# A two-branch attention kernel: 192 transposes moved from TensorE to a DMA queue, half sums on GpSimd, PV in sets of three, another start and end

## The chip, the cores and the metric

One core of a Trainium2 chip. The metric is the device time of one execution in microseconds (us), median of several executions. A change of less than 2% counts as no change.

## The reference, cut to what matters

Two attention branches read the same x (2048 x 512) and are mixed by a gate:

```python
# branch A: linear attention, 32 heads of 16
phi_q = concat([softmax(pq), softmax(-pq)])      # 32 features per head
phi_k = concat([softmax(pk), softmax(-pk)])
o = (phi_q @ (phi_k.T @ v)) / (phi_q @ phi_k.sum(tokens) + 1e-6)
# branch B: exact softmax attention, 32 heads of 16
p = softmax(q @ k.T * Dh ** -0.5);  o = p @ v
# out = g * (oA @ woA) + (1 - g) * (oB @ woB),  g = sigmoid((x * gate_w).sum(-1))
```

Branch B has 32 x 2048 x 2048 exponentials. The kernel cuts them in 2048 tiles of 128 x 512.

## The kernel before

ScalarE takes the exponentials of most tiles, in "slots" of three or two tiles (one activation for 1536 or 1024 columns). VectorE does the rest by bit tricks, partly with GpSimd. TensorE computes scores (`qk_mm`), PV, and the projections, and runs matmuls with zeros that are meant to hold its clock up. Branch A runs beside it. A planner inside the kernel (a list scheduler with a duration for each operation) fixes **the order of every engine** when the kernel is built. At run time each engine follows its order and waits on semaphores; if one entry waits, everything behind it on that engine waits (the lines of the changed kernel below show 3.84 us of such a wait on TensorE).

Transfers inside SBUF go to one queue, that of SyncE, at priority -40. The planner believes that each takes 0.07 us of the queue:

```python
def moves(kind, fn, n, reads, writes, name, lat=2.0):
    ...
    op = P.add("sp", 0.07 * n, -40, fn, reads=reads, writes=writes, name=name, sem=chain[kind][0], lat=lat)
```

Branch A's queries, 16 tiles of 128 tokens (cut). `fill` adds matmuls into a PSUM bank, `drain` what empties it:

```python
def q_rest(i, prio):
    b = i % 2
    mms = [... e.transpose(ap.bitcast(BF16)[:, 128*g:128*(g+1)], phiQ[:, b, 128*g:128*(g+1)], ident[:]) for g in range(8)]
    f, mm = fill(prio, mms, [("phiQ", b), "ident"], name=f"T{i}", ...)
    drain(f, mm, "dve", 0.69, prio, ... tensor_copy(phiQT[:, b, :, :], ap...), writes=[("phiQT", b)])
    for rnd in range(2):
        ...   # "N": 4 matmuls phiQT x kzbd (numerator and denominator), then VectorE writes oA
    mms = [... e.transpose(..., oA[:, b, 128*t:128*(t+1)], ident[:]) for t in range(KT)]       # KT = 4
    ...
    drain(f, mm, "dve", 0.42, prio, ... tensor_copy(oAT[:, i, :, :], ap...), writes=[("oAT", i)])
```

The normaliser of branch B uses SyncE's queue: after the last PV of a pair of heads the result leaves PSUM (tile Tf), its denominators go out and come back spread over the partitions (ld, Lq, lr, Rb), and GpSimd multiplies. In the trace oAT appears under the name phiK, whose memory it uses.

The softmax here doesn't subtract the row's maximum and nothing guards it: scores larger than these inputs give would overflow.

## Time and profile before

The profile that came with the kernel had caught an execution at about a quarter of TensorE's speed (the prediction shows its lines: matmuls of 512 columns stand 0.84 us apart). A second profile of the same kernel, taken with the first experiments, ran at full speed: there they stand 0.43 us apart in the warm-up and 0.22 us near the end (four from 778.05 to 778.91), at a mean granted clock of 0.993. First its page: span, busy times, busy tenths of ScalarE in 40 slices, the chain that ended last, and the group of the exponentials (its last columns are ScalarE's idle time before them and what ended it).

```profile
span 785.6 us, 15391 instructions
PE 726.2 (92%) x6304; PEld 227.5 (29%) x6304; DVE 681.8 (87%) x1125; ACT 762.4 (97%) x712; POOL 316.4 (40%) x273
ACT  5989999999999999999999999999999999999995
ACT 80%; PE 11%; DVE 5%; issue 1%; DMA 1%; SPq 1%; POOL 0%
L833 ACT ACTIVATE E_t<-psS 128x1536 bf16<-128x1536 f32 (+1 forms) x641 | 733.4, 1352 | 8.6 <-PE psS L741 6.8
```

ScalarE is busy from the first exponential to the last and owns 80% of the chain. So the prediction's reading, that ScalarE is the bound, holds at full speed. So do its durations of ScalarE: a 1536 and a 1024 back to back take 2.36 us here (from 10.82 on), 2.37 us at a quarter of TensorE's speed. Two pieces of notation: "SPq" is SyncE's queue, and "E_t" are the buffers that hold exponentials until PV has read them. The rest of this document uses four terms whose sum is the span: **head** (up to the first exponential), **floor** (ScalarE's own work, 756.5 us by the prediction's sum), **waits** (first to last exponential, less the floor) and **tail** (from the end of the last exponential). Here the first exponential starts at 10.82 and the last ends at 775.61, so these are 10.8 + 756.5 + 8.3 + 10.0 = 785.6.

### The profile page before, as it was taken

To read this page: it belongs to the slowest core of one execution; us is meant where nothing else is said; L and a number is where in the kernel's file an instruction comes from. 1 tells how busy PE (TensorE), PEld (TensorE's weight loads), DVE (VectorE), ACT (ScalarE), POOL (GpSimd) and SP (SyncE) were. 2 spreads that over 40 slices of the span, in tenths; PEclk is the share of its full clock that TensorE was granted. 3 is DMA by queue.
4 is the path that set the end of the run, shared out by engine and by line. 5 is a ranking of instruction groups with operands and counts; after the bars stand their busy time and mean duration, and the time that the engine had idled before them with its cause. 6 is when DMAs were issued, how large, how long until landed. Compare 5 with 4: busy or idle time off the path is not lost.

```text
span 1905.5 us, 15334 instructions
## 1 busy us (share of the span) xinstructions
PE 1865.0 (98%) x6247; PEld 289.4 (15%) x6304; DVE 695.2 (36%) x1125; ACT 821.8 (43%) x712; POOL 314.5 (17%) x273
## 2 busy tenths in 40 slices
PE   9999999999999999999999999999999999999999
PEld 3111112111211111212111111111111111111111
DVE  1332343333333333334333344443444443432431
ACT  2444444444444444444444444444444444443431
POOL 2010212112121121110222111120111202021200
DMA  4000000000000000100000000000000000000000
GB/s 111 2 3 12 6 4 6 4 9 4 4 6 3 9 3 2 31 3 9 4 4 6 3 10 4 5 7 2 9 4 9 4 4 12 9 7 9 13 9 14
DMA packets 37206, 18.01 MB, mean 9 GB/s; under 512 B 26584, under 2 KB 34136, under 8 KB 37136
## 3 DMA queue, kind: packets, MB, share of 16 engines
q1 hardware_dynamic: 35648, 16.36, 3.7%
q8 instruction: 49, 0.80, 0.2%
q10 hardware_dynamic: 1104, 0.66, 0.1%
q0 software_dynamic: 384, 0.02, 0.0%
q14 instruction: 21, 0.17, 0.0%
HBM read 7.87 MB, written 2.59 MB: 5 GB/s over the span
## 4 chain that ended last, share of the span: by engine, by line
PE 96%; DVE 2%; issue 2%; ACT 0%
PE psO L852 34%; PE psS L741 29%; PE psS L559 8%; PE psM L559 8%; PE psO L843 5%; PE psM L741 4%; PE psM L1097 1%; PE psS L597 1%; PE psS L609 1%; PE psM L609 1%; PE psM L477 1%; DVE Tx_t L799 1%; PE psS L1097 0%; PE psS L1122 0%; PE psM L1104 0%
## 5 line engine op out<-in xcount | busy, mean ns | idle before, releaser
L833 ACT ACTIVATE E_t<-psS 128x1536 bf16<-128x1536 f32 (+1 forms) x641 | 786.2, 1236 | 1009.4 <-PE psS L741 848.5
L741 PE MATMUL psS<-qz_t,kTB_t 32*128 32x512 bf16 x1828 | 659.3, 890 | 14.3 <-issue 3.1
L852 PE MATMUL psO<-E_t,vaug_t 128*32 128x512 bf16 x1602 | 539.7, 861 | 0.8 <-issue 0.8
L741 PE MATMUL psM<-qz_t,kTB_t 32*128 32x512 bf16 x220 | 189.0, 859 | 0.8 <-DVE Tx_t L799 0.8
L799 DVE TENSOR_SCALAR Tx_t<-psM 128x512 int16<-128x512 f32 x125 | 86.2, 690 | 219.3 <-PE psM L741 129.1
L741 PEld LDWEIGHTS psS<-qz_t,kTB_t 32*128 32x128 bf16 x1828 | 71.7, 103 | 603.2 <-issue 400.7
L822 POOL TENSOR_TENSOR Tx_t<-Tx_t,vA_t 128x512 bf16<-128x512 bf16 x88 | 99.3, 1155 | 363.7 <-DVE Ty_t L816 237.3
L799 DVE TENSOR_SCALAR Tx_t<-psS 128x512 int16<-128x512 f32 x125 | 86.1, 689 | 175.5 <-PE psS L741 152.8
L852 PE MATMUL psO<-Tx_t,vaug_t 128*32 128x512 bf16 (+1 forms) x250 | 135.1, 991 | 0.0
L852 PE MATMUL psO<-Ty_t,vaug_t 128*32 128x512 bf16 x250 | 123.6, 1009 | 0.0
L843 PE MATMUL psO<-xT_t,zero_t 128*32 128x512 bf16 x540 | 117.8, 820 | 0.0
L852 PEld LDWEIGHTS psO<-E_t,vaug_t 128*32 128x32 bf16 x1602 | 50.6, 99 | 298.4 <-issue 288.5
L822 POOL TENSOR_TENSOR oT_t<-oT_t,WoB_t 128x512 bf16<-128x512 bf16 x44 | 49.7, 1149 | 207.1 <-DVE oT_t L816 167.4
L1062 POOL TENSOR_TENSOR phiK_t<-EA_t,stat_t 128x1024 bf16<-128x1024 bf16 x16 | 30.8, 1928 | 249.7 <-DVE stat_t L1060 140.3
L852 PE MATMUL psO<-WAT_t,vaug_t 128*32 128x512 bf16 x152 | 69.8, 930 | 0.0
L852 PE MATMUL psO<-vA_t,vaug_t 128*32 128x512 bf16 x104 | 65.0, 962 | 0.0
L1062 POOL TENSOR_TENSOR phiQ_t<-EA_t,stat_t 128x1024 bf16<-128x1024 bf16 x16 | 30.8, 1926 | 187.8 <-DVE vA_t L814 80.8
L822 POOL TENSOR_TENSOR Tx_t<-Tx_t,WoB_t 128x512 bf16<-128x512 bf16 x32 | 36.2, 1151 | 147.1 <-DVE Ty_t L816 68.9
L559 PE MATMUL psS<-Wp_t,xT_t 128*128 128x512 bf16 x60 | 50.7, 971 | 1.5 <-DVE oT_t L816 0.5
L559 PE MATMUL psM<-xT_t,WB_t 128*128 128x512 bf16 x51 | 45.0, 1008 | 5.5 <-issue 4.8
L799 DVE TENSOR_SCALAR WAT_t<-psS 128x512 int16<-128x512 f32 x39 | 26.9, 690 | 63.0 <-PE psS L741 54.0
L559 PE MATMUL psM<-Wp_t,xT_t 128*128 128x512 bf16 x53 | 46.2, 1000 | 2.5 <-issue 1.5
(184 smaller groups left out, 1291.9 us busy)
## 6 DMA issues: line engine op xcount, KB each, us to landing
Rb_t<-lr SPq DMA_DIRECT2D x120, 32.0 KB, 1.8
qz_t<-qz_t SPq DMA_DIRECT2D x120, 16.0 KB, 1.8
Tf_t<-Tf_t SPq DMA_DIRECT2D x60, 32.0 KB, 2.0
out_dram<-WvA_t SPq DMA_DIRECT2D x14, 128.0 KB, 1.7
WB_t<-in_B_wqkv_dram SPq DMA_DIRECT2D x3, 384.0 KB, 4.7
WvA_t<-in_A_wqkv_dram SPq DMA_DIRECT2D x1, 512.0 KB, 4.0
WoA_t<-in_A_wo_dram SPq DMA_DIRECT2D x1, 512.0 KB, 3.5
WoB_t<-in_B_wo_dram SPq DMA_DIRECT2D x1, 512.0 KB, 4.7
```

The source lines that it names most:

```text
L477: ins = e.matmul(psM[:], lhsT=Ebuf[:, 0, 0:128], rhs=Ebuf[:, 0, 0:512], start=True, stop=True)
L559: return [lambda e, ap, i=i: e.matmul(ap, lhsT=lhs[i], rhs=rhs[i], start=(i == 0), stop=(i == len(lhs) - 1)) for i in range(len(lhs))]
L597: mms = [lambda e, ap, i=i, t=t: e.matmul(ap[:, 128 * i:128 * (i + 1)], lhsT=xT[:, t, NQ * c + 128 * i:NQ * c + 128 * (i + 1)], rhs=W_B[:, ...
L609: mms = [lambda e, ap, i=i, t=t: e.matmul(ap[:, 256 * i:256 * (i + 1)], lhsT=xT[:, t, NQ * c + 128 * (2 * hf + i):NQ * c + 128 * (2 * hf + ...
L741: return e.matmul(bank, lhsT=kT_B[32 * i:32 * i + 32, b // 8 % 2, 128 * kt:128 * (kt + 1)], rhs=qz[32 * i:32 * i + 32, b // 2 % 4, b % 2, ...
L799: ops.append(drain(f, mm, "dve", 0.70, d_prio(d), lambda e, ap, q=q: e.tensor_scalar(quarter(tb, q).bitcast(I16), ap, EXPB, 0.0, op0=ALU.a ...
L822: ops.append(P.add("pool", 1.1, d_prio(g["ts"][0]) - 5.0, lambda e, q=q: e.tensor_tensor(quarter(t4, q), quarter(t4, q), quarter(m4, q), A ...
L833: op = P.add("act", 0.051 + 0.4267 * n, 0.0, lambda e: e.activation(Ebuf[:, j // 2 % EPAIRS, 1536 * (j % 2):1536 * (j % 2) + 512 * n], psS ...
L843: ins = e.matmul(psO[32 * i:32 * i + 32, :], lhsT=zero[:], rhs=xT[:, 0, 0:NQ], start=False, stop=False, tile_position=(0, 32 * i), skip_gr ...
L852: return e.matmul(psO[32 * i:32 * i + w, :], lhsT=vaug[:, kt, o:o + w], rhs=rhs, start=start, stop=stop, tile_position=(0, 32 * i), skip_g ...
L1062: P.add("pool", 2.0, prio, lambda e: e.tensor_tensor(dst.rearrange("p (g f) -> p g f", f=DH), e3, stat[:, b, 1, :].unsqueeze(2).to_broadca ...
L1097: mms = [lambda e, ap, g=g: e.transpose(ap.bitcast(BF16)[:, 128 * g:128 * (g + 1)], phiQ[:, b, 128 * g:128 * (g + 1)], ident[:]) for g in ...
```

## The change

Intent: take tiles off ScalarE, give VectorE room for them (transposes and their copies go to the DMA queue, half of each feature sum to GpSimd), and shorten both ends. The diff, cut to its core:

```diff
-DN = (0, 10, 14, 14, 14, ...)        # sums to 446 tiles on VectorE
+DN = (0, 10, 14, 16, 14, ...)        # sums to 468
-ACTIVE = (0.64, 0.64, 0.58, 0.54)    # when zero matmuls are added
+ACTIVE = (1.0, 0.64, 0.62, 0.54)     # and zero matmuls into spare PSUM banks as well
+TR_LAT, TR_ISSUE = 3.0, 0.4          # what the planner is told of a DMA transpose
-PV_SETS, PV_FROM = 2, 0
+PV_SETS = 3                          # the PV of three slots in one merged piece
-K_AT, K_PACE, Q_AT, Q_PACE = 45.0, 13.0, 275.0, 14.0
+K_AT, K_PACE, Q_AT, Q_PACE = 45.0, 13.0, 275.0, 13.5
-D_AHEAD = 24.0                       # lead of VectorE's tiles, in slots
+D_AHEAD = 22.0
-        for _ in range(14):          # warm-up
+        for _ in range(6):           # and four more after the transposes of x
-    def moves(kind, fn, n, reads, writes, name, lat=2.0):
+    def moves(kind, fn, n, reads, writes, name, lat=2.0, each=0.07):
... q_rest: 8 + 4 TensorE transposes and two VectorE copies per tile go, in their place
+        moves(f"Te{b}", lambda e: [e.dma_start_transpose(phiQT[:, b, g, :], phiQ[:, b, 128 * g:128 * (g + 1)])
+                                   for g in range(8)], 8, [("phiQ", b)], [("phiQT", b)], ..., lat=TR_LAT, each=TR_ISSUE)
+        moves(f"Ue{b}", lambda e: [e.dma_start_transpose(oAT[:, i, t, :], oA[:, b, 128 * t:128 * (t + 1)])
+                                   for t in range(KT)], 4, ..., lat=TR_LAT, each=TR_ISSUE)
... phi: the sum over features starts with an addition of halves on GpSimd
-        P.add("dve", 1.22, prio, lambda e: e.tensor_reduce(stat..., e3, AX.X, ALU.add), ...)
+        P.add("pool", 1.15, prio, lambda e: e.tensor_tensor(half[:], e3[:, :, 0:8], e3[:, :, 8:16], ALU.add), ...)
+        P.add("dve", 0.66, prio, lambda e: e.tensor_reduce(stat..., half[:], AX.X, ALU.add), ...)
... the scaling after it is done in two halves
... out_last: tiles 14 and 15 get a partial sum early in SBUF; tiles 12 and 13 put seven of
    eight matmuls at priority -45 in place of 1000; only four matmuls stay for the very end
```

## The prediction

> **What bounds the kernel now.** I read four views, in this order: the page's busy line and chain, the timeline of the start, the groups of instructions by shape, and the timeline of the end. The first thing to see is that the profiled execution isn't the execution that was timed.
>
> ```profile
> span 1905.5 us, 15334 instructions
> PE 1865.0 (98%) x6247; PEld 289.4 (15%) x6304; DVE 695.2 (36%) x1125; ACT 821.8 (43%) x712; POOL 314.5 (17%) x273
> PE 96%; DVE 2%; issue 2%; ACT 0%
> ```
>
> The span is 1905.5 us, the timed median 786.79 us. The page makes TensorE the bound (98% busy, 96% of the chain). The start of the timeline says why:
>
> ```profile
> 1.19 11.55 PE L477 MATMUL psM<-E_t 128*128 128x512 bf16 x14 [1.19 <-DVE E_t L472]
> 4.17 0.26 PEld L477 LDWEIGHTS psM<-E_t 128*128 128x128 bf16 x1 [0.58 <-issue]
> 5.01 0.26 PEld L477 LDWEIGHTS psM<-E_t 128*128 128x128 bf16 x1 [0.58 <-issue]
> ```
>
> The warm-up matmuls stand 5.01 - 4.17 = 0.84 us apart, so a stream of 512 columns runs at 512 / 0.84 = 610 columns per us. The end of the same profile has the same step. TensorE ran the whole profiled execution at about a quarter of its speed, although the page prints a granted clock of 1.0. TensorE work is 1865 / 0.84 = 2220 streams. [...] TensorE isn't the bound in what is timed. ScalarE doesn't depend on that clock, so its durations can be used:
>
> ```profile
> L833 ACT ACTIVATE E_t<-psS 128x1536 bf16<-128x1536 f32 x320 | 464.0, 1450 | 790.3 <-PE psS L741 657.8 <-PE psM L741 128.8 <-PE psO L852 3.7
> L833 ACT ACTIVATE E_t<-psS 128x1024 bf16<-128x1024 f32 x321 | 328.4, 1023 | 219.1 <-PE psS L741 190.7 <-PE psM L741 24.1 <-PE psO L852 2.4
> L1053 ACT ACTIVATE EA_t<-psS 128x512 bf16<-128x512 f32 x34 | 18.4, 595 | 18.0 <-PE psS L559 18.0
> L1053 ACT ACTIVATE EA_t<-psM 128x512 bf16<-128x512 f32 x30 | 16.3, 596 | 11.4 <-PE psM L559 11.4
> 303.41 2.37 ACT L833 ACTIVATE E_t<-psS 128x1536 bf16<-128x1536 f32 x2 [3.19 <-PE psS L741]
> ```
>
> Durations sum to 821.8 us, more than the timed span, so successive activations must overlap. The last line shows how much: a 1536 and a 1024 back to back take 2.37 us together, not 1.450 + 1.023 = 2.473, so each step is 0.105 us shorter than its duration: 1.345, 0.918 and 0.49 us. **ScalarE's floor**: 320 x 1.345 + 321 x 0.918 + 64 x 0.49 = 430.4 + 294.7 + 31.4 = 756.5 us of 786.8. That is the bound. The other 30 us are, by estimate, a head of about 11.6 us (warm-up, four transposes, Q, K and their copies, first scores), a tail of about 9.5 us after the last exponential, and about 9 us of waits between. DVE has 695.2 us of durations, and its timeline overlaps successive ones by a similar 0.1 us, so it is occupied nearer 75%.
>
> [...]
>
> **The change part by part.**
>
> *More tiles off ScalarE.* The tuple of tiles per block done on VectorE sums to 446 before and 470 after. Of 2048 tiles ScalarE keeps 1602, then 1578; dealt in threes and twos that is 320 + 321, then 316 + 315 exponentials. ScalarE saves 4 x 1.345 + 6 x 0.918 = **10.9 us**, all on the path.
>
> *VectorE pays and is paid.* These rows carry what is removed:
>
> ```profile
> L1058 DVE TENSOR_REDUCE stat_t<-EA_t 128x64 f32<-128x1024 bf16 x32 | 38.7, 1211 | 9.3 <-ACT EA_t L1053 9.3
> L1100 DVE COPY phiQT_t<-psM x11: 691/691/692, 899.7 to 1511.6; 128x1024 bf16<-128x1024 bf16 x11
> L1125 DVE COPY phiK_t<-psS x11: 424/425/425, 1020.5 to 1529.8; 128x512 bf16<-128x512 bf16 x11
> L822 POOL TENSOR_TENSOR Tx_t<-Tx_t,vA_t 128x512 bf16<-128x512 bf16 x88 | 99.3, 1155 | 363.7 <-DVE Ty_t L816 237.3 <-DVE vA_t L814 85.7 <-DVE WAT_t L816 36.0
> ```
>
> The transposed copies go: 16 x 0.69 + 16 x 0.425 = 17.8 us. The sum over features reads half as much: I estimate 0.68 us in place of 1.211[...], 32 x 0.53 = 17.0 us. Against that stand 24 tiles x 0.69 = 16.6, about 7 us of bit masks and 7 us of products (groups of four go from 98 to 108, groups of two from 27 to 19; the number of groups multiplied on GpSimd stays at 49). VectorE's sum falls by 34.8 - 30.4, some 4 us: unchanged, and beside the path.
>
> *GpSimd* gets 32 half sums, by the last row about 1.15 us each: +37 us on 314.5, and some more for splitting the scaling in two. GpSimd and the locked VectorE operations (about 235 us, 14 us more after) then take about 600 of 770 us where they took 549 of 787. Tighter, not a bound.
>
> *TensorE* loses 16 x 12 = 192 small transposes[...], and PV in sets of three slots packs 7 or 8 tiles into two passes over the four column groups, where each slot had its own pass: about 641 passes become 430[...]. It gains 24 score tiles and 48 PV terms, mostly riding beside others. The first ACTIVE threshold goes from 0.64 to 1.0, so many more zero matmuls fill its gaps (540 in the trace now, 135 sets of four[...]). They are meant to hold the clock up.
>
> *SyncE's queue* gets 192 transposes. The twelve of x in the trace take 15.59 us to issue, 1.30 us each, with four times the rows. Between 0.33 and 1.3 us each makes 63 to 250 us of 770, with 3.4 us to land; a tile of the linear branch has about 16 us. Hidden, unless the normalising transfers queue behind it.
>
> *Head.* [...] The x tiles land near 4.4 us (issued from 0.74 us, about 3 us to land), so this and the reordered loads save about **2 us**, on the path.
>
> *Tail.* In the end of the timeline the last vector chain is short and the output projection long:
>
> ```profile
> 1882.06 0.72 DVE L957 STREAM_TRANSPOSE Tf_t<-psO 128x512 f32<-128x512 f32 x1 [12.46 <-PE psO L852]
> 1883.56 0.71 DVE L967 STREAM_TRANSPOSE oT_t<-Rb_t 128x512 bf16<-128x512 bf16 x1
> 1899.84 2.68 PE L559 MATMUL psS<-WoB_t,oT_t 128*128 128x512 bf16 x3
> ```
>
> The chain needs 2.2 us; 25 output matmuls stand in the same stretch[...]. [...] The change sums two tiles early and leaves four matmuls to the end: **2.8 us** saved.
>
> *Sum*: 786.8 - 10.9 - 2 - 2.8 = 771.1 us, if the 9 us of waits stay. Fewer passes of PV in front of the next scores and a steadier clock should take a few of them; I put 3 us. **768 us**.
>
> **The rivals.** (a) *TensorE becomes the path.* [...]a merged PV piece is two or three passes long; the ring of scores gives only one exponential (0.9 to 1.3 us) of slack. For it: the new threshold, and an order fixed beforehand. Against it: [...]fewer passes. If a sixth of 631 exponentials waited 0.2 us longer, +21 us: 785 to 795. (b) *The linear branch or VectorE's locked chain gets late*: DMA transposes or GpSimd's halves delay tiles, and scores wait for PSUM banks. For it: 3.4 us landings where a copy took 0.69; against it: a pace of 16 us per tile. It would make 775 to 785. (c) *The clock matters more than I think*: if much of the 9 us, and some of the head, is half-speed TensorE, the filling removes it, and 757 to 763 comes out.
>
> **Range and chances.** The three terms on the path are well founded on ScalarE (10.9) and softer at both ends (4.8 with perhaps 2 of error); the waits may move by 5 either way, more under (a). I take 758 to 780. The limit of 2% is 771.05 us, close to the sum without any gain in waits, so the chance of faster is only moderately above half: 0.60, within 2% 0.36, slower 0.04.
>
> **What would show it.** Exponentials must number 316 and 315 with unchanged durations, the reduction must be near 0.68 us, GpSimd's half sum near 1.15 us. If the changed profile is again at a quarter speed, its span tells only how many TensorE streams there are, and it may well be longer than 1905 us from zero matmuls while the timed run is shorter. If it is at full speed, ScalarE should be over 95% busy with few waits on scores. I'm wrong if ScalarE's waits in a full-speed run are much more than 9 us between head and tail, or if head and tail don't shrink by some 5 us.

## The result, and the profile after

The changed kernel took **886.87 us** (median; 883.86 to 891.75, four runs) against 785.71 for the kernel before in the same rounds: ratio 1.1296, 95% interval 1.123 to 1.1362. A ratio here is always the mean time of one kernel's runs over that of the other's in the same rounds, so it isn't quite the ratio of the medians quoted. Executions over 1.5% slower than the fastest of the same kernel are left out of the means. The result is correct. It is 12.96% slower, where the prediction had 2.3% faster. The page of the changed kernel, at full speed from 20 to 360 us (granted clock 1.00; 0.919 over the span); the row "ACT" again in 40 slices, "PEclk" the granted clock in tenths:

```profile
span 884.6 us, 17783 instructions
PE 776.7 (88%) x7308; PEld 235.5 (27%) x7370; DVE 683.3 (77%) x1120; ACT 760.3 (86%) x703; POOL 360.3 (41%) x337
ACT  5999999999999999986795668657775966999996
PEclk9999999999999999997696879878886997999999
ACT 43%; PE 22%; SPq 21%; DVE 6%; DMA 4%; issue 3%; POOL 0%; DVEq 0%
L853 ACT ACTIVATE E_t<-psS 128x1536 bf16<-128x1536 f32 x632 | 729.8, 1311 | 100.2 <-PE psS L761 85.6
L1149 PE MATMUL psS<-kzbd_t,phiQT_t 128*128 128x68 bf16 x60 | 5.6, 231 | 40.3 <-DMA phiQT_t<-phiQ_t 40.3
```

ScalarE has no more work than predicted (its sum fell), but now idles 100.2 us before exponentials. A queue, SPq, has 21% of the chain, where it had 1%. TensorE's largest wait stands in the last row: the N matmuls of branch A wait for phiQT. A table by stretch shows where (columns: stretch, its length, then busy time and count of PE, PEld, DVE, ACT and POOL, granted clock, DMA share, GB/s):

```profile
20.00:360.00 340.00, 328.28 (x3291) 105.68 (x3315) 301.92 (x467) 339.23 (x320) 157.17 (x139) 1.00 0.10 25
360.00:745.00 385.00, 301.30 (x2678) 82.77 (x2695) 259.22 (x462) 279.34 (x259) 136.78 (x124) 0.82 0.13 26
```

Up to 360 us ScalarE is busy 339.23 of 340 us. Between 360 and 745 it idles 385 - 279.34 = 105.7 us. That stretch holds the sixteen query tiles of branch A, and with them all 192 transposes. One of the waits, from the timeline (columns: start, length, engine; in brackets the idle time before it and what ended it):

```profile
393.35 10.53 SPq L1146 DMA_TRANSPOSE phiQT_t<-phiQ_t  x8
...
405.19 0.38 PE L1149 MATMUL psS<-kzbd_t,phiQT_t 128*128 128x68 bf16 x4 [3.84 <-DMA phiQT_t<-phiQ_t]
405.50 0.61 PE L761 MATMUL psS<-qz_t,kTB_t 32*128 32x512 bf16 x3
...
406.16 2.37 ACT L853 ACTIVATE E_t<-psS 128x1536 bf16<-128x1536 f32 x2 [3.40 <-PE psM L761]
```

Eight transposes of one tile hold the queue for 10.53 us. TensorE reached the N matmuls that need them 3.84 us before the data was there. The next scores stand behind these in TensorE's fixed order, and the exponential behind the scores: ScalarE idles 3.40 us.

Adding up all lines of SyncE's queue in the timeline from 360 to 745 gives 327.9 us, 85% of the stretch: 192 transposes hold it 247.0 us, **1.29 us each**, and 143 plain transfers about 0.57 us each, 81 us together. (A line of several instructions includes the short gaps between them. The instructions alone come to 239.9 + 76.9 = 316.8 us, 82%, and a transpose to 1.25 us. In the kernel before, the same stretch has 104.9 us of plain transfers alone, 27%.) Per tile of branch A that is 12 x 1.29 + 81 / 16 = 15.5 + 5.1 = 20.5 us, in a plan that starts a tile about every 16 us (in the batched kernel below, the first transposes of the sixteen tiles stand 16.0 us apart in the mean; here it became 23.5). The planner was told 12 x 0.4 + a few times 0.07.

There is a second half to the loss. In this stretch the granted clock is 0.82 in the mean: by the trace's clock records it is 0.5 for 139.9 of the 385 us. All 15 falls to 0.5 come within 4 us of a stretch of over 1 us (1.92 to 8.61 us) in which TensorE stood idle. Of ScalarE's 105.7 us of idle time, 50.7 fall where TensorE stands idle too, 45.7 where TensorE works at the half clock, and 9.2 elsewhere (counted from the trace). So a late tile is paid for twice by this count: while TensorE waits, and in the slow stretch that follows. No run separates the two.

In the four terms: head 12.2, floor 746.5 (316 x 1.345 + 316 x 0.918 + 64 x 0.49), waits 117.1, tail 8.9. The whole loss is in the waits.

### The profile page after: what moved, and what is told of

Same layout as the page of the kernel before. It is cut to its first block, busy times and chain, and to the rows that moved or that the text cites. A ratio compares the mean times of both kernels' runs of the same rounds, so it can differ in the third digit from the quotient of the medians.

```text
span 884.6 us, 17783 instructions
## 1 busy us (share of the span) xinstructions
PE 776.7 (88%) x7308; PEld 235.5 (27%) x7370; DVE 683.3 (77%) x1120; ACT 760.3 (86%) x703; POOL 360.3 (41%) x337
## 4 chain that ended last, share of the span: by engine, by line
ACT 43%; PE 22%; SPq 21%; DVE 6%; DMA 4%; issue 3%; POOL 0%; DVEq 0%
ACT E_t L853 41%; SPq L1146 14%; PE psS L761 7%; PE psO L873 5%; SPq L1167 4%; PE psO L863 3%; DMA phiQT_t<-phiQ_t 2%; PE psS L579 2%; ACT EA_t L1095 2%; SPq L970 2%; PE psM L579 2%; DVE Tx_t L819 1%; DMA lr<-rd_t 1%; DVE vA_t L834 1%; PE psM L761 1%
## 5 line engine op out<-in xcount | busy, mean ns | idle before, releaser
L853 ACT ACTIVATE E_t<-psS 128x1536 bf16<-128x1536 f32 x632 | 729.8, 1311 | 100.2 <-PE psS L761 85.6
L761 PE MATMUL psS<-qz_t,kTB_t 32*128 32x512 bf16 x1823 | 298.8, 404 | 20.5 <-ACT E_t L853 13.8
L863 PE MATMUL psO<-xT_t,zero_t 128*32 128x512 bf16 x1732 | 163.0, 404 | 0.0
L873 PE MATMUL psO<-E_t,vaug_t 128*32 128x512 bf16 x1580 | 147.4, 403 | 0.2 <-DVE vaug_t L625 0.2
L761 PE MATMUL psM<-qz_t,kTB_t 32*128 32x512 bf16 x225 | 89.9, 399 | 3.8 <-DVE oA_t L1164 3.5
L1100 POOL TENSOR_TENSOR half_t<-EA_t 128x512 f32<-128x512 bf16 x32 | 37.2, 1164 | 93.6 <-ACT EA_t L1095 36.6
L973 POOL TENSOR_TENSOR oT_t<-Tf_t,Rb_t 128x512 bf16<-128x512 f32 x15 | 19.3, 1284 | 103.5 <-DMA Rb_t<-lr 64.6
L863 PEld LDWEIGHTS psO<-xT_t,zero_t 128*32 128x32 bf16 x1732 | 40.2, 96 | 71.6 <-issue 61.3
L873 PE MATMUL psO<-Tx_t,vaug_t 128*32 128x512 bf16 x244 | 48.2, 408 | 0.0
L842 POOL TENSOR_TENSOR WAT_t<-WAT_t,vA_t 128x512 bf16<-128x512 bf16 x28 | 31.7, 1156 | 39.0 <-DVE WAT_t L836 15.7
L836 DVE TENSOR_SCALAR Ty_t<-Tx_t 128x2048 int16<-128x2048 int16 (+1 forms) x64 | 46.4, 728 | 0.1
L1108 POOL TENSOR_TENSOR phiK_t<-EA_t,stat_t 128x512 bf16<-128x512 bf16 x32 | 33.9, 1058 | 30.7 <-DVE oT_t L839 10.8
L873 PE MATMUL psO<-Ty_t,vaug_t 128*32 128x512 bf16 x244 | 36.0, 420 | 0.0
```

Of the source, the lines that this page charges most:

```text
L761: return e.matmul(bank, lhsT=kT_B[32 * i:32 * i + 32, b // 8 % 2, 128 * kt:128 * (kt + 1)], rhs=qz[32 * i:32 * i + 32, b // 2 % 4, b % 2, ...
L836: add(0.72 if full else 0.45, lambda e: e.tensor_single_scalar(shaped(si16, si16), shaped(ti16, si16), 0x7F80, ALU.bitwise_and), tk, [g["s ...
L842: ops.append(P.add("pool", 1.1, d_prio(g["ts"][0]) - 5.0, lambda e, q=q: e.tensor_tensor(quarter(t4, q), quarter(t4, q), quarter(m4, q), A ...
L853: op = P.add("act", 0.051 + 0.4267 * n, 0.0, lambda e: e.activation(Ebuf[:, j // 2 % EPAIRS, 1536 * (j % 2):1536 * (j % 2) + 512 * n], psS ...
L863: ins = e.matmul((psO if bank is None else bank)[32 * i:32 * i + 32, :], lhsT=zero[:], rhs=xT[:, 0, 0:NQ], start=bank is not None, stop=ba ...
L873: return e.matmul(psO[32 * i:32 * i + w, :], lhsT=vaug[:, kt, o:o + w], rhs=rhs, start=start, stop=stop, tile_position=(0, 32 * i), skip_g ...
```

## The experiments

**Theory Q** (the expectations call it Theory S). The queue is the cause: a DMA transpose holds it 1.29 us, so a tile's data comes late, and since all orders are fixed the lateness goes through TensorE to ScalarE. **Rivals:** the other parts of the change do the harm (zero matmuls in front of scores, PV in larger pieces, GpSimd's new work); or DMA transposes disturb other things, whatever their queue time.

Whatever is edited, the planner lays out all orders anew. Two variants therefore differ in many places, and differences of 1 or 2% can come from that alone (seen below). Only where the text says so is the order the same.

### A profile of the kernel before at full speed

> The unchanged kernel, to get a profile of it at full TensorE speed, if the profiler gives one. Both theories: 783 to 788 us timed. If the profile is at full speed, ScalarE is over 93% busy throughout, no stretch is slower than the others by more than a few per cent, and SyncE's queue is busy for less than 40% of any stretch. If it is again at a quarter of the speed, the span is near 1905 us and nothing more is learnt.

No edit (run e0_before). 787.42 us timed, one execution, span 785.6. Its lines were shown above. ScalarE is the bound, with 8.3 us of waits.

### The changed kernel with the transposes back on TensorE

> The changed kernel with one part undone: the 192 DMA transposes of the linear branch go back to TensorE transposes with VectorE copies; all else of the change stays. Theory S (the DMA transposes fill SyncE's queue, 192 x 1.29 us = 247 us in a stretch of 385 us, and TensorE, whose order is fixed, waits there): the stretch runs at the rate of the others, about 106 us of ScalarE idle time go, 765 to 790 us. Rival T (TensorE is overfilled by zero matmuls and merged PV pieces): those are all still there, so it stays above 840 us. Rival G (GpSimd's added half sums hold up VectorE's tiles): likewise above 840 us.

```diff
-        moves(f"Te{b}", ... dma_start_transpose ...)
+        ... fill(... e.transpose ...); drain(... tensor_copy(phiQT ...))       # as before, also for oAT
```

Run e1_pe_transpose: 797.91 us, ratio 1.015 (1.0117 to 1.0183). That is above the 765 to 790 expected of Theory S and far below the 840 of the rivals. 89 of the 101 us of loss are gone with the DMA transposes, so the other parts of the change aren't the cause of the large loss. They don't gain here either: TensorE is busy 97%, and ScalarE waits 16.9 us in 8 places for buffers of exponentials that PV has yet to read.

### The kernel before with the 192 DMA transposes alone

> The kernel before with that one part alone: the linear branch transposed by 192 DMA transposes (same code, same planned 0.4 us each), nothing else of the change. Theory S: it alone costs some 100 us, 860 to 910 us. Rivals T and G: it has neither the new threshold nor the half sums, so it stays within 780 to 800 us.

```diff
-        ... e.transpose ..., tensor_copy ...
+        moves(f"Te{b}", ... 8 dma_start_transpose ..., lat=TR_LAT, each=TR_ISSUE)     # 3.0, 0.4 as in the change
+        moves(f"Ue{b}", ... 4 dma_start_transpose ...)
```

Run e2_before_dma: 904.67 us, ratio 1.1523 (1.1492 to 1.1554). This one part makes a loss of 119 us without any of the rest. Its page and its largest waits of ScalarE and TensorE (us in total, times, longest):

```profile
ACT  5999999999999999865877666697676769999995
ACT E_t L834 <- PE psS L742: 107.5, 66, 8.5
PE psS L1101 <- DMA phiQT_t<-phiQ_t: 34.0, 6, 8.0
PE psM L1101 <- DMA phiQT_t<-phiQ_t: 22.5, 7, 7.9
```

The same hole in the same stretch, and the same waits for phiQT.

### The changed kernel with the transposes in 32 instructions

> The changed kernel with the same transposes in 32 instructions in place of 192: one of 128x1024 for the features, one of 128x512 for the result, each planned at 1.3 us of the queue. The loads of x, four times as large as one of the 192, took 1.30 us each. Theory S with a cost per instruction: 32 x 1.3 = 42 us of the queue, no stretch stalls, 765 to 790 us. Theory S with a cost per 128x128 block: 192 x 1.3 us stay, 870 to 900 us. Rivals T and G: above 840 us.

```diff
-TR_LAT, TR_ISSUE = 3.0, 0.4
+TR_LAT, TR_ISSUE = 3.0, 1.3
-        moves(..., lambda e: [e.dma_start_transpose(phiQT[:, b, g, :], phiQ[:, b, 128*g:128*(g+1)]) for g in range(8)], 8, ...)
+        moves(..., lambda e: e.dma_start_transpose(phiQT[:, b, :, :], phiQ[:, b, :]), 1, ...)
-        moves(..., lambda e: [e.dma_start_transpose(oAT[:, i, t, :], oA[:, b, 128*t:128*(t+1)]) for t in range(KT)], 4, ...)
+        moves(..., lambda e: e.dma_start_transpose(oAT[:, i, :, :], oA[:, b, :]), 1, ...)
```

Run e3_batched: 784.71 us, ratio 0.9995 (0.9967 to 1.0024), and correct. The same bytes are transposed by the same means, but one instruction takes 128 x 1024 or 128 x 512 in place of 128 x 128. Its page, and two entries of SyncE's queue:

```profile
PE 757.2 (97%) x7322; PEld 233.2 (30%) x7322; DVE 686.6 (88%) x1120; ACT 754.7 (97%) x703; POOL 361.7 (46%) x337
ACT  5999999999999999999999999999999999999795
ACT 57%; PE 29%; DVE 12%; issue 1%; DMA 1%; SPq 0%
404.40 1.27 SPq L1146 DMA_TRANSPOSE phiQT_t<-phiQ_t  x1
416.40 1.20 SPq L1166 DMA_TRANSPOSE phiK_t<-oA_t  x1
```

An instruction with eight times the data holds the queue as long (1.27 us) as each of the eight did. (Over all of them the medians are 1.27 us for 128 x 1024, 1.23 for 128 x 512, and 1.23 for 128 x 128 in the changed kernel.) So **the cost is one of instructions, not of bytes**. The 32 instructions take 42.0 us of the queue where the 192 took 239.9 (247.0 with the gaps), the hole is gone, and 102 us with it. The spans differ by 884.6 - 781.6 = 103.0 us, and the waits term by 117.1 - 13.4 = 103.7. The edit also tells the planner the true cost, 1.3 us; that this alone doesn't mend the 192 is seen in e4_told below. The rival "transposing by DMA disturbs something" is out as far as bytes go; whether many small ones disturb is asked again below.

But this isn't the predicted 768 either. The next runs ask why. One thing is visible at once: the row "ACT" has a 7 in its third slice from the end, and the table by stretch shows TensorE at half its clock there:

```profile
725.90:739.60 13.70, 13.70 (x87) 2.86 (x88) 7.68 (x14) 9.00 (x9) 6.32 (x6) 0.50 0.21 32
```

TensorE is busy all of the 13.7 us (every matmul that starts from 726.75 to 739.40 is of the form 32*128 or 128*32), the granted clock is 0.50, and ScalarE idles 13.70 - 9.00 = 4.7 us. In the 3.4 us before this stretch (the shortest stretch at 0.5 in the clock records of the changed kernel is 3.41 us long) TensorE was busy 2.71 us, with idle gaps of 0.24 and 0.32 us among the rest. The stretch belongs to the order: e6_tail below, which has the same order there, has 13.7 us at 0.50 as well, from 725.0.

### The 192 transposes, with the planner told their cost

> The changed kernel with its 192 DMA transposes kept, and only the planner's figures corrected to what the trace shows: 1.27 us of the queue for a transpose in place of 0.4, 0.55 us for a plain transfer in place of 0.07. Every engine's order is planned anew. Theory S1 (what costs is that the planner, told 0.4, put the waiting matmuls too early in TensorE's fixed order; the queue itself has room, 328 of 385 us): it comes down to 785 to 810 us. Theory S2 (the queue has too little room: 15.5 us of transposes and some 4.6 us of other transfers per tile of the linear branch, against a pace of about 15.5 us per tile): the branch gets late however it is planned, and 830 to 880 us remain.

```diff
-TR_LAT, TR_ISSUE = 3.0, 0.4
+TR_LAT, TR_ISSUE = 3.0, 1.27
-    def moves(kind, fn, n, reads, writes, name, lat=2.0, each=0.07):
+    def moves(kind, fn, n, reads, writes, name, lat=2.0, each=0.55):
```

Run e4_told: 961.22 us, ratio 1.2243 (1.2213 to 1.2273): worse, and above what either theory expected. The largest waits:

```profile
ACT E_t L853 <- PE psO L873: 178.4, 4, 68.2
POOL oT_t L973 <- DMA Rb_t<-lr: 143.4, 3, 55.4
```

The planner now gives the queue to whatever is ready first. The transposes are created earlier and have the same priority as the normalising transfers, so these starve: GpSimd waits up to 55.4 us for Rb, the buffers behind it don't come free, PV has no place to start, and ScalarE stands up to 68.2 us. So truth in the plan alone doesn't mend it. A tile's 20.5 us of queue don't fit in 16 us, so something has to give way; that it is the normalising transfers because of the equal priority is read from the planner's code, and no run changes the priority alone.

### The batched kernel with the old filling of zeros

> The run with batched transposes, with the old thresholds for zero matmuls (0.64, 0.64, 0.58, 0.54) and none on the spare banks, so a third of the zero matmuls or fewer. Rival T in its weak form (the fill costs some of the missing 17 us): 770 to 778 us. If the fill is there for the clock and does it: 790 us or more, with more stretches of low granted clock. If neither matters: 781 to 788 us.

```diff
-ACTIVE = (1.0, 0.64, 0.62, 0.54)
+ACTIVE = (0.64, 0.64, 0.58, 0.54)
-    P.idle, P.misc = zero_mm, MISC
+    P.idle, P.misc = zero_mm, []
```

Run e5_old_fill: 781.88 us, ratio 0.9969 (0.9935 to 1.0003; one of the six runs, 791.47, counts as slow and isn't in the ratio), with 656 zero matmuls in place of 1732. Within what a new order does, the filling neither gains nor costs. This answers one half of the prediction's rival (a): zeros ahead of scores aren't what was lost. The other half, PV in merged pieces, stands in all these runs and wasn't undone.

### The batched kernel with a mended end

> The run with batched transposes, its order the same up to the last twenty rows of TensorE: the seven early matmuls of tile 13 come after the last PV piece, not before it (they hold it up by about 1.5 us there), and the 40 zero matmuls after the last real one are gone (they end at 781.3 us of a span of 781.6). If both are on the path, as I think: 1.5 to 2.5 us less than with batched transposes, about 782.5 us. If the last transfers set the end anyway: within 1 us of it.

In the batched kernel the predicted gain at the end was missing: its tail is 10.2 us against 10.0 before. Its end shows why:

```profile
771.54 1.04 PE L579 MATMUL psM<-WoA_t,phiK_t 128*128 128x512 bf16 x4
772.41 0.81 PE L579 MATMUL psM<-WoB_t,oT_t 128*128 128x512 bf16 x3
773.15 0.39 PE L873 MATMUL psO<-E_t,vaug_t 128*32 128x512 bf16 x2
```

The seven matmuls of output tile 13, at the new priority -45, stand ahead of the last PV, on which the whole end depends; and zero matmuls run beside the last copies up to 781.27. The edit keeps the order (the first 7344 of TensorE's 7405 instructions are the same) but for some twenty entries at the end and the zero matmuls there:

```diff
-                if pick is None and e == "pe" and not zero_ok and t > 20.0 and active < ACTIVE[0]:
+                if pick is None and e == "pe" and not zero_ok and left > 40 and t > 20.0 and active < ACTIVE[0]:
-            f, mm = fill(-45, mms[:7], ..., after=last_d1 + o_mms)
+            f, mm = fill(-45, mms[:7], ..., after=last_d1 + o_mms + (pv_last[-1:] if i else []))
```

Run e6_tail: 779.88 us, ratio 0.9928 (0.9902 to 0.9954). The tail is 7.3 us, so the predicted 2.8 us (10.0 to 7.2) were there, but not in the change as it was written. The median is 4.8 us below that of the batched kernel, more than the 1.5 to 2.5 expected. Between the two profiles the span falls by 3.7 us: the tail by 2.9, the head by 1.8, while the waits rise by 1.1. The edit doesn't touch the head, so that part is chance (see "The head" below).

### The kernel before with 32 batched transposes alone

> The kernel before with the linear branch transposed by 32 batched DMA transposes, nothing else of the change. If the transposes are harmless once they take 42 us of the queue in place of 247: 780 to 790 us, and no gain, since the VectorE copies they replace were beside the path. If a DMA transpose does harm beside the queue's time (landing late, or slowing other transfers): above 800 us.

The edit is that of the batched kernel, made in the kernel before. Run e7_before_batched: 801.99 us, ratio 1.0223 (1.0198 to 1.0248), on both sides of the 2% limit, so unclear by the rule. It is outside the expected 780 to 790, and just inside the "above 800" that was expected if a DMA transpose does harm beside the queue's time. Compared with the 904.67 of the 192, 103 us are gone again. Of the 16 us that the span has more than before, 11.6 are waits. From 590 to 612 us the granted clock is 0.61 and ScalarE is busy 14.79 of 22 us, and near 750 and 777 it waits for PV. The first of these begins with a DMA transpose that landed late:

```profile
594.79 0.38 PE L1100 MATMUL psS<-kzbd_t,phiQT_t 128*128 128x68 bf16 x4 [2.68 <-DMA phiQT_t<-phiQ_t]
```

The clock falls to 0.5 at 594.0, while TensorE waits here, and stays there for 17.1 us. So a batched transpose can still come late in a given order, and a part of the 2% is that. The rest I put down to laying out the order anew, which isn't shown; it is the reason not to read small differences between variants.

### The 192 transposes, told, in another order of the queue, and with more time

> The changed kernel with its 192 single transposes kept, but paced so that the queue has room: a tile of the linear branch is started every 21.8 us by estimate in place of about 15.5 (its queue time is 12 x 1.29 + about 4.6 = 20 us), the planner is told 1.27 us per transpose and 0.55 us per plain transfer, and a normalising transfer that is ready goes ahead of a transpose. Theory (the queue of SyncE was overfull: 20 us of issue per 15.5 us of pace): the waits for phiQT and for the normalising transfers nearly vanish and the time falls from 887 to 785-825, although every one of the 192 transposes is still there. Rival (single transposes by DMA harm by themselves, by their landing times or by what they disturb on the buffers and the other engines): the time stays above 850, with waits behind phiQT or phiK spread over the whole stretch.

```diff
 (on top of e4_told)
-KG_AT, KG_PACE, QG_AT, QG_PACE = 40.0, 13.0, 270.0, 14.0
+KG_AT, KG_PACE, QG_AT, QG_PACE = 40.0, 13.0, 270.0, 19
-K_AT, K_PACE, Q_AT, Q_PACE = 45.0, 13.0, 275.0, 13.5
+K_AT, K_PACE, Q_AT, Q_PACE = 45.0, 13.0, 275.0, 19
+    # the two transposing moves at priority -39, behind the normalising transfers at -40
```

Run e8_paced: 820.21 us, ratio 1.0441 (1.0387 to 1.0494), inside the 785 to 825 expected and far from 850. All 192 single transposes are still there (128 + 64, median 1.232 us each) and hold the queue 243.1 us without gaps. In 370 to 770 the queue is even fuller than in the changed kernel: 343.8 of 400 us, 86%, counted by the instructions alone, against 82%. Yet ScalarE idles 400 - 362.57 = 37.4 us where it idled 105.7, and the clock records have 37.5 us at 0.5 where they had 139.9. So neither the transposes themselves nor a full queue costs most of the time; work that was planned sooner than the queue can deliver does. No wait of TensorE for phiQT is left among those of 0.2 us or more in all, and none of GpSimd for Rb. Most of what is left of ScalarE's waits comes behind PV:

```profile
ACT E_t L853 <- PE psO L873: 31.3, 7, 8.5
```

Three things changed at once here (costs told, order of the queue, pace), and the first alone made it worse, so the runs don't say how the other two share the gain. The 35 us that remain above the kernel before aren't explained by a run either.

### Three candidates for a better kernel

> A candidate: batched transposes, the end in the mended order (e6_tail), and the thresholds of the zero matmuls as in the kernel before, without zeros on spare banks. If the filling is useless, as e5_old_fill made likely, the time is that of e6_tail within 0.5%, 776-784. If the filling hinders by standing ahead of scores, 772-777. If it is needed for the clock once the end is mended, above 786.

> A candidate: as e6_tail, with VectorE's tiles planned one us further ahead (23 in place of 22). If VectorE's tiles come late at times and hold back PV and with it the banks, some us less: 773-778. If they don't, the time of e6_tail within 0.5%, 776-784; differences below that may be the new order alone.

> As e6_tail, with the lead of VectorE's tiles as in the kernel before the change (24 slots of the planner; the change made it 22, e10_ahead took 23; the unit is slots, not us as e10_ahead's expectation said). So this undoes one more part of the change. Theory A (the shorter lead was a loss): 768-774, no worse than e10_ahead. Theory B (e10_ahead was a lucky order and any new order lands within some 1% of e6_tail): anywhere in 773-788; the profile then shows again a stretch of low clock or waits on scores that e10_ahead lacks. The two overlap near 773; outside it the time decides.

```diff
 (each on top of e6_tail)
 e9_tail_oldfill:  ACTIVE = (0.64, 0.64, 0.58, 0.54) and P.misc = []
 e10_ahead:        D_AHEAD = 23.0      (22.0 in the change, 24.0 before it)
 e11_ahead24:      D_AHEAD = 24.0
```

| run | us, median (range) | ratio to before (95%) |
|---|---|---|
| e9_tail_oldfill | 780.54 (778.37-788.78) | 0.9951 (0.9902-1.0) |
| e10_ahead | **772.52** (771.86-774.22) | **0.9826** (0.9792-0.9861) |
| e11_ahead24 | 783.34 (781.16-785.15) | 0.9974 (0.995-0.9998) |

(The lead is counted in slots of the planner; the expectation of e10_ahead says us by mistake.) The filling again makes no clear difference. With a lead of 23 slots the kernel beats both: 1.7% under the kernel before (span 769.7). The interval, 0.9792 to 0.9861, lies on both sides of 0.98, so by the 2% rule the verdict is unclear; it just misses the 773 to 778 that was expected if a longer lead helps. Its page:

```profile
ACT  5999999999999999999999999999999999999996
PEclk9999999999999999999999999999999999999999
L853 ACT ACTIVATE E_t<-psS 128x1536 bf16<-128x1536 f32 x632 | 724.3, 1344 | 3.6 <-PE psS L761 2.7
```

ScalarE waits 3.6 us before exponentials in all; there is no stretch at half clock near 730. One slot more of lead lands at 783.34 with waits of 15.7. It lands where Theory B put it. So the expectation that a longer lead as such helps isn't borne out, and a lead of 23 isn't shown to be better than 22 by a mechanism. What is shown is that the same parts in another order range from 3 to 16 us of waits.

## Why the prediction was wrong

The four terms, in us. First exponential and end of the last one are from each timeline; "predicted" is the prediction's own arithmetic on its estimate of before:

| | head | floor | waits | tail | span |
|---|---|---|---|---|---|
| before | 10.8 | 756.5 | 8.3 | 10.0 | 785.6 |
| predicted for after | 9.6 | 745.6 | 6 | 6.7 | 768 |
| after | 12.2 | 746.5 | **117.1** | 8.9 | 884.6 |
| e3_batched | 11.5 | 746.5 | 13.4 | 10.2 | 781.6 |
| e6_tail | 9.7 | 746.5 | 14.5 | 7.3 | 777.9 |
| e10_ahead | 11.9 | 746.5 | 3.2 | 8.1 | 769.7 |

**The step that failed** is the one on SyncE's queue: "Between 0.33 and 1.3 us each makes 63 to 250 us of 770, with 3.4 us to land; a tile of the linear branch has about 16 us. Hidden, unless the normalising transfers queue behind it." The prediction's own sign of being wrong, waits of much more than 9 us, came true with 117.1. The transposes of the trace then in hand took 1.30 us each; I allowed 0.33 because they have four times the rows, which supposes that the queue's time goes with the data. It doesn't (e3_batched: 1.27 us for eight times the data). The cost was 1.29 us, the upper end. And 250 us were set against 770 us, though all of them fall in the sixteen tiles of one stretch. The sum to make was the one per tile: 12 x 1.30 = 15.6 us for transposes alone against 16 us, before a single other transfer. Its numbers all stood in the prediction. The exception named there, normalising transfers queueing behind, came true as well: GpSimd waits 64.6 us for Rb where it waited 24.9.

**Rival (b)** named the mechanism ("DMA transposes or GpSimd's halves delay tiles, and scores wait for PSUM banks") but gave it 775 to 785. It argued from the landing time of one transfer against the pace of a tile. That counts a lateness once; a queue that needs 20.5 us per tile where the plan gives 16 gets later with every tile, sixteen times 4.5 = 72 us by estimate. In the traces the chain of fixed orders passed this on, 105.7 us of ScalarE idle in the stretch. The lag is larger than 72: a tile starts every 23.5 us where the batched kernel has 16.0, 15 x 7.5 = 113 us over the fifteen steps. What the estimate lacks is at least in part the half clock after each wait (45.7 us of ScalarE's idle time). So **rival (c)**, the clock, had a share too, though as a consequence of the queue, and opposite in sign to the gain that (c) had in mind. That it began with the wait for phiQT in TensorE's order, rather than for PSUM banks, is shown by the lines of the changed kernel.

**ScalarE** was right: 316 + 316 exponentials (the prediction has 315: it sums the tuple of VectorE's tiles to 470, and it is 468, so 22 tiles moved and not 24), floor 746.5, so 10 us saved for 10.9 predicted. The bound of the kernel before was right too; in e10_ahead it is again all that counts.

**TensorE**: that it isn't the bound was my estimate, made from a profile at a quarter of its speed; e0_before shows it, with 11% of the chain for TensorE and 80% for ScalarE. Its 726.2 us (92%) on that page don't measure its work: a matmul of 512 columns is counted with 0.38 us from 781.07, and the next ones start 0.22 us after it. That PV terms and scores ride beside others is seen there too: eight PV matmuls start as four at 772.00 and four at 772.22, and three score matmuls take 0.39 us together from 771.67.

**VectorE and GpSimd** were right. These rows of the changed kernel, by shape, answer to the prediction's 1.15 and 0.68 us:

```profile
L1100 POOL TENSOR_TENSOR half_t<-EA_t 128x512 f32<-128x512 bf16 x32 | 37.2, 1164 | 93.6 <-ACT EA_t L1095 36.6 <-DVE Tx_t L839 20.3 <-DVE WAT_t L839 12.8
L1102 DVE TENSOR_REDUCE stat_t<-half_t 128x64 f32<-128x512 f32 x32 | 21.6, 676 | 3.5 <-POOL half_t L1100 3.3
```

VectorE's sum stayed (681.8 before, 683.3 after), as predicted to within 6 us.

**The head** was predicted to save 2 us. Over the ten profiles with the new start the first exponential comes at 11.0 us in the mean (9.65 to 12.15), over three with the old one at 11.6 (10.82 to 12.03): perhaps 0.6 us, inside the scatter. The warm-up did become shorter (the old one ended at 6.0 us), but in the ten profiles TensorE waits until 5.35 to 5.92 us for the second pair of x tiles, so this wait took the warm-up's place. The scatter goes with the clock: in four of the ten the clock records are at full from 4.3 to 5.4 us on, and the first exponential comes at 9.65 to 9.98; in six only from 9.1 to 10.4 on, and it comes at 11.5 to 12.2. With the old start they are at full from 4.5 to 7.0 us on. Whether the shorter warm-up is what makes the clock come late isn't shown.

**The tail** of 2.8 us was right in size (it was an estimate; the time of the output matmuls in it wasn't shown), but the change as written didn't have it: 10.2 in e3_batched. e6_tail found the entries in the way, and has it (7.3).

**The waits**, once the queue is mended, were predicted to fall by 3 and rise by 5 in e3_batched. Part of that is the stretch at half clock (4.7 us from 725.9 to 739.6). e10_ahead has 3.2. Prediction and best case are 3 us apart, but neither the filling with zeros (e5_old_fill, e9_tail_oldfill) nor the lead of VectorE's tiles explains which order gets which; why the clock falls in some orders stays open.

**Rival (a)** (TensorE in the way, 785 to 795) isn't what happened to the changed kernel, but it describes e1_pe_transpose: 797.91 us, TensorE 97% busy, 16.9 us of waits behind PV. With the parts of this change, putting the transposes back on TensorE isn't the mend; fewer, larger DMA transposes are.

Single transposes, as planned, then account for the whole loss of 101 us in the changed kernel (102 us between it and the batched one). In the kernel before, batching takes away 103 of 119 us. The route is the queue, as e3_batched and e8_paced show; how much of the time is waiting and how much the half clock that follows isn't separated. The gain that the rest was to bring is there in one order of the plan (772.52 us, 4.5 above the prediction, and unclear by the 2% rule) and not in others.

## What to carry to other kernels

Moving work to a DMA queue moves it to an engine that has a capacity of its own (SyncE's queue was 85% taken here from 360 to 745 us): count its instructions, multiply by what one holds the queue in the trace at hand, and compare that with the time between two uses, stage by stage and not over the whole run. A wait on TensorE can cost more than its length: look at the granted clock after it (in the changed kernel ScalarE idled 50.7 us beside an idle TensorE, and 45.7 us beside a TensorE at the half clock). Where the cost of a transfer is per instruction, batch: eight transposes in one instruction took the queue's time of one (medians of 1.27 and 1.23 us). And when orders are fixed at build time, a planner that is told a third of a cost (0.4 for 1.29) plans waits into every engine; but telling it the truth helps only if the work then fits and if what others wait for goes first.

## What the runs show of the queue and the clock

- A transpose inside SBUF holds SyncE's queue 1.25 us in the mean (changed kernel, 360 to 745 us), a plain transfer in the same stretch 0.43 to 0.65 us by kind. The transposes of x from DRAM hold the queue 1.26 us (median).
- In these runs this time doesn't depend on the size of the transpose: medians of 1.23 us for 128 x 128, 1.27 for 128 x 1024, 1.26 for the 512 x 128 ones of x from DRAM. Batching eight into one saved 102 us of 887.
- One profile here was at a quarter of TensorE's speed (0.84 us for 512 columns, against 0.22 in e0_before), while that profile printed a granted clock of 1.0. After a gap of 1.92 us the changed kernel has a clock of 0.5 from 382.5 us, and e3_batched fell to 0.5 after gaps of 0.24 and 0.32 us in the 3.4 us before. Why it then stays there for 13.7 us, in which TensorE shows no gap, wasn't settled.
